# A first weight load issued third on GpSimd's queue, and the head's steps in a new order

## The chip, the cores and the metric

The program runs on one core of one Trainium2 chip. The metric is device time in microseconds (us) of one execution, smaller is better. Besides the plain times there is one execution taken by the hardware profiler; times inside it are counted from the start of its span.

## The reference, cut to what matters

There are two stages. The first is a sparse causal attention over 4 batches of 8 heads, 768 positions and 64 dimensions a head. Keys are taken in 24 chunks of 32. Each query gets an upper bound for each chunk from the chunk's smallest and largest key, keeps the 6 chunks with the highest bound, and attends to those alone:

```python
ub = np.sum(np.maximum(q[:, :, :, None, :] * k_min[:, :, None, :, :], q[:, :, :, None, :] * k_max[:, :, None, :, :]), axis=-1)
ub = np.where(causal, ub, -1000000000.0)
top_chunks = np.argsort(ub, axis=-1)[..., -top_k:]
mask = sel & (pos[:, None] >= pos[None, :])
scores = np.where(mask, scores, -1000000000.0)
attn = np.exp(scores - max);  attn = attn / sum;  out = attn @ v
```

The second stage is a soft mixture of experts over the 3072 x 512 result `x`: `logits = x @ phi` (32 slots); a softmax over all rows gives each slot its input, eight experts of two layers (`w1` 512 x 1024, relu, `w2` 1024 x 512) turn four slots each, and a softmax over the slots mixes the slot outputs back to the rows:

```python
d = softmax(logits, axis=0);  slot_input = d.T @ x
slot_out[e] = np.maximum(slot_input[e] @ w1[e], 0.0) @ w2[e]
return (softmax(logits, axis=1) @ slot_out).astype(np.float32)
```

## The kernel before, in words

Heads are worked on in 16 pairs, four to a batch. For a pair, q and k are transposed on TensorE (`transposes`, line 225), copied out of PSUM (`evac_T`, line 235), the chunk minima and maxima are reduced on VectorE (`kmin`, `kmax`, lines 244 and 250), spread over the two heads (`heads`, line 256; on VectorE as step `bd`, on GpSimd as step `bdp`), and multiplied with the negative and positive part of q (`qneg` line 264, `qpos` lines 272 and 274) to the upper bound (`ubound`, lines 284 and 294). `select` (lines 305 to 308) finds the sixth highest of each query with VectorE, with a small copy on GpSimd; the not-selected marks are transposed (`ns_transposes` line 316, `evac_ns` line 324) and added as a large negative number to the scores by matmuls (`scores`, lines 334 and 344). ScalarE takes the exponential (`expo`, line 358), in six groups `ex:0` to `ex:5`; groups 0, 1 and 4 have 1024 columns, the others 768. GpSimd zeroes what lies above the diagonal (`mask`, line 368). The product with v, the normalisation and the experts' stages come behind.

The program's order is written by hand. Pair 0, and the first steps of pairs 1 and 2, are the string `HEAD` (line 638), which is read word by word by `head` (line 640): each word issues its instructions, and each engine works its own instructions off in the order in which the words stand. The words: `w:n` issues n matmuls of 512 columns on a constant (`warm`, line 215) whose result nobody reads; `kd`, `ka`, `qd`, `qa` cast the two heads of pair 0's k and q on VectorE or ScalarE; `trk:i`, `trq:i` transpose, `evk:i`, `evq:i` copy out; `caus`, `qgrp`, `squad`, `identf`, `once` make constants on GpSimd, `schunk` on VectorE; `spreada` and `spreadp` fill the mask table on ScalarE and on GpSimd; `lk:i`, `lq:i` load k or q of the pairs i and i+1, `lv:i` loads v of pair i, `lw` the next of the expert weights, `phi` the slot matrix; `sc:g`, `ex:g`, `mk:g` are the score groups of pair 0. After `HEAD` a loop over pairs 1 to 15 reads a like string for each pair.

All loads but two are issued by GpSimd's queue, convert f32 to bf16 on their way, and land in the order in which they were issued; the two of pair 0 come from SyncE's queue (line 184) and don't convert. Loads of pair 1 and the constant `ident` stand ahead of `HEAD` (lines 185 to 190), as do the loads of pairs 2 and 3 (`load(2, ...)`, lines 202 and 203). Fourteen weight matrices of 1024 KB (`load_w`, line 150) are spread over the head and the loop; the last two matrices come as eight half pieces of 256 KB (`load_w_half`, line 160), the last four of them issued when the attention is done (line 859). The results leave by SyncE's queue: half of the columns (`out_half(m, 1, ...)`, line 1054) once the experts' first half is ready, the other half and the rest (line 1062 on) after the last weight pieces have been used (`last_expert_out`, line 1006).

Of the kernel before, what the change touches and what calls it, by code (L numbers as in the profile page):

```python
# [59 lines left out]
def kernel(  # L60
# [50 lines left out]
    identf = static.tile([P, P], F32, name="identf")  # L111
    ones_sq = static.tile([P, P], BF16, name="ones_sq")
    NJ = NQT // 2
    caus = static.tile([P, 1, 8], BF16, name="caus")
    qgrp = static.tile([P, 4, CH], BF16, name="qgrp")
    smask = static.tile([P, 2, NQT, 4, CH], BF16, name="smask")
    squad = static.tile([P, 2, 2, NCHUNK], BF16, name="squad")
    schunk = static.tile([P, 2, NCHUNK, 1], BF16, name="schunk")
# [23 lines left out]
    def load_w(i):  # L142

        if i < E:
            src = moe_w1[i].rearrange("(a p x) f -> p a (x f)", p=P, x=2)
            dst = w_sb[i].rearrange("p (a f) -> p a f", a=NDG // 2)
        else:
            src = moe_w2[LATE[i - E]].rearrange("(a p x) d -> p a (x d)", p=P, x=4)
            dst = w_sb[i].rearrange("p (a f) -> p a f", a=NFG // 4)
        nc.gpsimd.dma_start(out=dst, in_=src)  # L150
# [12 lines left out]
    def load(i, nm, n=1):  # L163

        b, j = divmod(i, NPB)
        t = ring[nm][i // 2 % 3][:, 2 * (i % 2):2 * (i % 2 + n)]
        src = {"k": k, "q": q}[nm][b, 2 * j:2 * (j + n)]
        nc.gpsimd.dma_start(out=t, in_=src.rearrange("h (p g) d -> p h (g d)", p=P))
        for x in range(n):
            st[nm, i + x] = t[:, 2 * x:2 * x + 2]  # L170
# [12 lines left out]
    for t, src in zip(stage, (k, q)):  # L183
        nc.sync.dma_start(out=t, in_=src[0, :2].rearrange("h (p g) d -> p h (g d)", p=P))
    load(1, "k")
    load(1, "q")
    nc.gpsimd.affine_select(
        out=ident, in_=ident, compare_op=ALU.not_equal, fill=1.0, base=0,
        pattern=[[-1, P]], channel_multiplier=1,
# [387 lines left out]
    once = static.tile([P, 8], BF16, name="once")  # L577
# [5 lines left out]
    def setup(name):  # L583
# [39 lines left out]
        elif name == "lw":  # L623
            load_w(LW.pop(0))
        else:
            return False
        return True

    LW = [0, 1]
    EVAC = {"evk": "k", "evq": "q"}  # L630
    CASTS = {"kd": (0, "k", 0, nc.vector.tensor_copy), "ka": (0, "k", 1, nc.scalar.copy),
             "qp": (1, "q", 0, nc.gpsimd.tensor_copy), "qd": (1, "q", 0, nc.vector.tensor_copy),
# [2 lines left out]
          "bdp": lambda i: heads(i, nc.gpsimd),  # L635
          "sel": select, "ns": ns_transposes, "evns": evac_ns, "lv": load_v}

    HEAD = """w:6 w:1 ka kd lv:0 caus qd qgrp trk:0 w:1 evk:0 qa trq:0 kmin:0 w:4 kmax:0 w:1 evq:0 lk:4 qsn:0 bd:0 squad schunk w:1 trk:1:s qsp:0 ub:0 w:1 spreada w:2 spreadp lw evk:1 w:1 sel:0 w:1 trq:1:s evq:1 ns:0 evns:0 sc:0 kmin:1 lv:1 kmax:1 lq:4 sc:1 lk:6 w:2 w:1 qsp:1 qsn:1 ex:0 sc:2 mk:0 w:1 ex:1 sc:3 ex:2 mk:2 bd:1 trk:2 ub:1 ex:3 mk:1 sel:1 sc:4 sc:5 evk:2 lq:6 kmin:2 mk:3 ex:4 trq:2 w:1 mk:4 once lv:2 ns:1 w:1 evns:1 w:1 evq:2 lw w:1 kmax:2 phi identf bd:2 qsn:2 ex:5 qsp:2"""

    def head(what):  # L640
        name, *arg = what.split(":")
        if setup(name):
            return
        if name in CASTS:
            cast(*CASTS[name])
            return
        i = int(arg[0])
        if name == "w":
            warm(i)
        elif name in ("trk", "trq"):  # L650
            runs = ((0, 3), (3, NQT)) if what == "trk:0" else ((0, NQT),)
            transposes(i, name[2], runs, (p_sc, "sc") if what == "trk:0" or arg[1:] else (p_tp, "tp"))
        elif name in EVAC:
            evac_T(i, EVAC[name], *((nc.scalar.copy, nc.vector.tensor_copy) if what == "evk:0" else ()))
        elif name in DO:
            DO[name](i)
        elif name in ("lk", "lq"):
            load(i, name[1], 2)
        elif name == "sc":
            scores(0, i)  # L660
        elif name == "ex":
            expo(0, i, False)
        elif name == "mk":
            mask(0, i)

    for what in HEAD.split():
        head(what)
# [442 lines left out]
```

## Time and profile before

| | us |
|---|---|
| median of 3 runs (lowest, highest) | 156.52 (156.43, 158.02) |
| the profiled execution's own time | 156.65 |
| its span | 154.9 |
| TensorE busy | 137.1 (89%) |
| ScalarE busy | 121.4 (78%) |
| VectorE busy | 120.3 (78%) |
| GpSimd busy | 97.3 (63%) |
| loads and stores, sum | 33.31 MB at a mean of 215 GB/s |

The profiled execution's time is 1.75 us longer than its span; the span is what the views divide up. A row of the timeline has start, duration, engine, line, operation, output<-inputs, shapes and count; in square brackets stands the idle time before it and what ended it. A row of DMA issues ends with the time from issue to landing. A row of the table of stretches has the stretch, its length, then the busy time of PE, PEld, DVE, ACT and POOL with their numbers of instructions, the granted clock of TensorE, the DMA engines' busy share (above 1 where transfers of one engine overlap) and GB/s moved.

### The profile page before, as it was taken

Reading aid. Unit: us, or ns where it says so; the run is one execution under the profiler, and the core shown is the slowest. Engines: PE = TensorE matmul, PEld = TensorE weight load, DVE = VectorE, ACT = ScalarE, POOL = GpSimd, SP = SyncE. Lnnn points to the kernel's source line nnn. Section 1 sums busy time; section 2 is a strip of 40 time slices with the busy share of each in tenths; the row PEclk is TensorE's granted clock in tenths of the full one; section 3 lists DMA queues with packets and bytes.
Section 4 is the critical chain, followed back from the end, with each engine's and each line's share of the span. In section 5 each row is a group of like instructions: output and inputs, shape, how many; then the busy total and the mean of one; then the engine's idle time right before and its main releaser. Section 6 shows DMA issues by size and latency. Waiting matters only on the chain.

```text
span 154.9 us, 6107 instructions
## 1 busy us (share of the span) xinstructions
PE 137.1 (89%) x2512; PEld 91.4 (59%) x2513; DVE 120.3 (78%) x445; ACT 121.4 (78%) x167; POOL 97.3 (63%) x200
## 2 busy tenths in 40 slices
PE   7999999999999999999999899999989899576700
PEld 2544566766767685766768566668768557353200
DVE  5866988989899998999999999999567532449800
ACT  3578999999999999999999989999977231527700
POOL 6976698965975898896649848793785950000000
PEclk9999999999999999999999999999999999999995
DMA  5999999999999999999999999999999999998995
GB/s 175 178 187 212 199 193 193 218 176 196 211 215 191 198 209 186 198 207 214 199 194 200 203 209 196 205 184 218 209 200 214 210 200 193 163 328 305 378 406 230
DMA packets 46171, 33.31 MB, mean 215 GB/s; under 512 B 26304, under 2 KB 41664, under 8 KB 46144
## 3 DMA queue, kind: packets, MB, share of 16 engines
q0 software_dynamic: 41328, 25.86, 115.2%
q1 hardware_dynamic: 4816, 7.08, 12.5%
q8 instruction: 19, 0.31, 0.7%
q14 instruction: 8, 0.07, 0.1%
HBM read 52.49 MB, written 6.29 MB: 379 GB/s over the span
## 4 chain that ended last, share of the span: by engine, by line
PE 65%; POOL 8%; DMA 7%; DVE 6%; ACT 5%; issue 4%; DVEq 0%; POOLq 0%; ACTq 0%
PE sc_ps L334 14%; PE at_ps L382 13%; PE sc_ps L344 10%; PE tr_ps L225 8%; DMA w_half<-in_moe_w_dram 7%; PE xT_ps L404 4%; PE warm_ps L215 3%; PE ub_ps L284 3%; ACT e_sb L358 3%; PE ns_ps L316 3%; DVE o_sb L1030 2%; POOL w_half L160 1%; POOL e_sb L368 1%; POOL v_t L174 1%; ACT o_sb L1027 1%
## 5 line engine op out<-in xcount | busy, mean ns | idle before, releaser
L358 ACT ACTIVATE e_sb<-sc_ps 128x1024 bf16<-128x1024 f32 (+2 forms) x96 | 83.2, 932 | 4.5 <-PE sc_ps L344 4.3
L368 POOL TENSOR_SCALAR_AFFINE_SELECT e_sb<-e_sb 128x256 bf16<-128x256 bf16 x96 | 37.8, 414 | 15.3 <-ACT e_sb L358 15.1
L334 PE MATMUL sc_ps<-qT,kT 64*128 64x384 bf16 (+3 forms) x260 | 37.5, 306 | 0.7 <-ACT e_sb L358 0.6
L344 PE MATMUL sc_ps<-nsT,smask 64*128 64x384 bf16 (+2 forms) x296 | 37.6, 284 | 0.1
L382 PE MATMUL at_ps<-v_t,e_sb 128*128 128x65 bf16 x630 | 26.0, 194 | 0.9 <-DVE x_sb L395 0.8
L382 PEld LDWEIGHTS <-e_sb 128*128 128x128 bf16 x630 | 22.1, 97 | 5.1 <-issue 3.9
L305 DVE MAX8 mx<-ub_ps 128x8 f32<-128x8 f32 (+1 forms) x192 | 16.9, 165 | 5.9 <-PE ub_ps L294 5.9
L334 PEld LDWEIGHTS <-kT 64*128 64x128 bf16 x260 | 13.5, 93 | 8.4 <-issue 1.8
L174 POOL DMA_DIRECT2D v_t<-in_v_dram x16 | 17.1, 1066 | 1.5 <-PE sc_ps L344 1.3
L344 PEld LDWEIGHTS <-smask 64*128 64x128 bf16 x296 | 14.9, 95 | 3.1 <-issue 0.4
L395 DVE TENSOR_TENSOR x_sb<-at_ps,inv 128x768 bf16<-128x768 f32 (+3 forms) x18 | 15.6, 869 | 0.6
L244 DVE TENSOR_REDUCE mm<-kT 128x24 bf16<-128x768 bf16 x16 | 15.1, 944 | 0.1
L250 DVE TENSOR_REDUCE mm<-kT 128x24 bf16<-128x768 bf16 x16 | 15.1, 943 | 0.0
L235 ACT COPY qT<-tr_ps 128x768 bf16<-128x768 bf16 x16 | 13.0, 814 | 2.2 <-PE tr_ps L225 2.2
L235 ACT COPY kT<-tr_ps 128x768 bf16<-128x768 bf16 (+1 forms) x16 | 12.7, 794 | 0.6 <-PE tr_ps L225 0.6
L150 POOL DMA_DIRECT2D w_sb<-in_moe_w_dram x14 | 10.1, 721 | 0.1
L415 DVE COPY xT_sb<-xT_ps 128x768 bf16<-128x768 bf16 (+1 forms) x16 | 8.6, 535 | 1.9 <-PE xT_ps L404 1.9
L215 PE MATMUL warm_ps<-ones_sq 128*128 128x512 bf16 x27 | 9.0, 458 | 1.1 <-DVE ones_sq L180 1.1
L284 PEld LDWEIGHTS <-qpn 128*128 128x128 bf16 x192 | 6.0, 96 | 4.5 <-issue 3.3
L404 PE MATMUL xT_ps<-ident,x_sb 128*128 128x128 bf16 x96 | 8.4, 220 | 0.0
L284 PE MATMUL ub_ps<-bd,qpn 128*128 128x48 bf16 x192 | 7.9, 184 | 0.4 <-issue 0.3
L1027 ACT ACTIVATE o_sb<-oh_ps,inv_a 128x256 f32<-128x256 f32 x12 | 5.0, 470 | 3.5 <-PE oh_ps L1041 2.8
(171 smaller groups left out, 222.5 us busy)
## 6 DMA issues: line engine op xcount, KB each, us to landing
w_sb<-in_moe_w_dram POOLq DMA_DIRECT2D x14, 1024.0 KB, 18.4
out_dram<-o_sb SPq DMA_DIRECT2D x14, 256.0 KB, 3.8
v_t<-in_v_dram POOLq DMA_DIRECT2D x16, 192.0 KB, 15.3
out_dram<-o_sb SPq DMA_DIRECT2D x5, 512.0 KB, 4.4
w_half<-in_moe_w_dram POOLq DMA_DIRECT2D x8, 256.0 KB, 11.8
k_in<-in_k_dram POOLq DMA_DIRECT2D x5, 384.0 KB, 13.4
q_in<-in_q_dram POOLq DMA_DIRECT2D x5, 384.0 KB, 12.2
w_sb<-in_k_dram POOLq DMA_DIRECT2D x2, 384.0 KB, 11.4
```

Source lines behind the costliest of these rows:

```text
L174: nc.gpsimd.dma_start(out=v_t[i % NV][:, :, :, :D], in_=v[b, 2 * j:2 * j + 2].rearrange("h (g p) d -> p h g d", p=P),)
L235: copy(t.rearrange("d (p g) -> d p g", g=NQT)[:, :, g0:g1], ps.rearrange("d g p -> d p g"),)
L244: nc.vector.tensor_reduce(mm[:, 0, 0, :], kT, axis=AX.X, op=ALU.min)
L250: nc.vector.tensor_reduce(mm[:, 1, 0, :], kT, axis=AX.X, op=ALU.max)
L284: nc.tensor.matmul(o, lhsT=qpn[:, x, t * P:(t + 1) * P], rhs=bd[:, x], start=(t == 0 and x == 0), stop=False,)
L305: nc.vector.max(mx[:, a, :], ub[:, a, :max(8, 4 * t + 4)])
L334: nc.tensor.matmul(ps[:, h, c:c + w], lhsT=kT[r, kg * P:(kg + 1) * P], rhs=qT[r, qs], start=True, stop=False,)
L344: nc.tensor.matmul(ps[:, h, c + (f - t0) * P:c + (l - t0) * P], lhsT=smask[r, x, kg].rearrange("p a b -> p (a b)"), rhs=nsT[r, (f - x * NJ ...
L358: nc.scalar.activation(e[:, :, :w], st.pop(("scps", i, g))[:, :, :w], func=ACT.Exp, scale=scale)
L368: nc.gpsimd.affine_select(out=e[:, :, c:c + P], in_=e[:, :, c:c + P], compare_op=ALU.is_ge, fill=0.0, base=0, pattern=[[0, 2], [1, P]], ch ...
L382: nc.tensor.matmul(o, lhsT=st["e", i, g][:, h, c:c + P], rhs=v_t[i % NV][:, h, kg, :D + 1], start=(kg == 0), stop=(kg == t),)
L395: nc.vector.tensor_tensor(st["x", b][:, t0:t1, 2 * j:2 * j + 2, :].rearrange("p t h d -> p h t d"), at[:, :, :, :D], inv.broadcast_to([P, ...
```

## The change

One weight load is moved from the word `lw` in the middle of `HEAD` to the third place of GpSimd's queue, and the words of `HEAD` get a new order, which also has more `w:` words, `bdp:1` in the place of `bd:1`, and the word `lw` once instead of twice.

```diff
     load(1, "k")
     load(1, "q")
+    load_w(0)
     nc.gpsimd.affine_select(
         out=ident, in_=ident, compare_op=ALU.not_equal, fill=1.0, base=0,
...
-    LW = [0, 1]
+    LW = [1]
...
-    HEAD = """w:6 w:1 ka kd lv:0 caus qd qgrp trk:0 w:1 evk:0 qa trq:0 kmin:0 w:4 kmax:0 w:1 evq:0 lk:4 qsn:0 bd:0 squad schunk w:1 trk:1:s qsp:0 ub:0 w:1 spreada w:2 spreadp lw evk:1 w:1 sel:0 w:1 trq:1:s evq:1 ns:0 evns:0 sc:0 kmin:1 lv:1 kmax:1 lq:4 sc:1 lk:6 w:2 w:1 qsp:1 qsn:1 ex:0 sc:2 mk:0 w:1 ex:1 sc:3 ex:2 mk:2 bd:1 trk:2 ub:1 ex:3 mk:1 sel:1 sc:4 sc:5 evk:2 lq:6 kmin:2 mk:3 ex:4 trq:2 w:1 mk:4 once lv:2 ns:1 w:1 evns:1 w:1 evq:2 lw w:1 kmax:2 phi identf bd:2 qsn:2 ex:5 qsp:2"""
+    HEAD = """w:1 kd w:3 ka w:7 trk:0 qa caus qgrp qd lv:0 lk:4 trq:0 evk:0 w:2 w:2 squad evq:0 w:2 qsp:0 w:1 kmin:0 kmax:0 bd:0 lv:1 w:1 qsn:0 w:1 trk:1:s trq:1 ub:0 w:1 schunk evq:1 spreada spreadp w:1 w:2 lq:4 evk:1 sel:0 w:3 ns:0 evns:0 qsn:1 sc:0 w:1 sc:1 ex:0 kmin:1 w:1 w:1 ex:1 w:1 qsp:1 kmax:1 w:3 bdp:1 trk:2 lk:6 evk:2 ub:1 sc:2 ex:2 sc:3 sel:1 identf mk:0 w:1 ex:3 once kmin:2 w:1 sc:4 kmax:2 trq:2 mk:2 lq:6 mk:1 ex:4 lv:2 evq:2 sc:5 mk:4 w:1 mk:3 ns:1 evns:1 bd:2 w:1 qsn:2 lw phi ex:5 qsp:2"""
```

## The prediction

> **What bounds the kernel now.** I read the page first, then the table of stretches, then the waits at the end. From the page, DMA busy share in 40 slices and GB/s:
>
> ```profile
> DMA  5999999999999999999999999999999999998995
> GB/s 175 178 187 212 199 193 193 218 176 196 211 215 191 198 209 186 198 207 214 199 194 200 203 209 196 205 184 218 209 200 214 210 200 193 163 328 305 378 406 230
> ```
>
> The stretches (last columns: granted clock, DMA share, GB/s):
>
> ```profile
> 2.00:137.90 135.90, 130.27 (x2472) 88.20 (x2471) 111.35 (x422) 114.08 (x155) 96.42 (x196) 1.00 1.35 203
> 140.00:141.00 1.00, 0.79 (x7) 0.40 (x5) 0.93 (x4) 0.93 (x3) 0.00 (x0) 1.00 0.50 177
> 141.00:153.00 12.00, 3.98 (x26) 1.64 (x24) 5.61 (x10) 4.41 (x8) 0.00 (x0) 0.89 1.02 383
> ```
>
> The reader is to see two bounds side by side. The DMA engines have work from 2.0 us to the last weight piece at 137.9, and then write results; TensorE is busy for 130.27 of those 135.90 us. Where they meet is seen in the chain in order of time and in TensorE's timeline:
>
> ```profile
> 127.27 10.62 DMA w_half<-in_moe_w_dram
> 132.54 0.29 PE L1006 MATMUL so_ps<-w_half,hT_pad 128*32 128x256 bf16 x4 [0.76 <-DMA w_half<-in_moe_w_dram]
> 137.94 0.29 PE L1006 MATMUL so_last<-w_half,hT_pad 128*32 128x256 bf16 x4 [0.32 <-DMA w_half<-in_moe_w_dram]
> ```
>
> TensorE waits for weight pieces twice, 0.76 and then 0.32 us. So the arithmetic may come 0.76 + 0.32 = 1.08 us later before the end moves, and coming earlier gains nothing while the loads last until 137.9. Behind that there is no slack: between 140 and 141 the DMA share is 0.50, the results' stream itself waits there for the arithmetic.
>
> **The change: the load stream.** A load lands in the order of issue, and the queue is already full when the moved load was issued. GpSimd's timeline and, below it, time from issue to landing of the loads of pairs 2 and 3 (k, then q), of v of pair 0 and of w:
>
> ```profile
> 3.21 0.79 POOL L168 DMA_DIRECT2D k_in<-in_k_dram  x1
> 3.97 0.77 POOL L168 DMA_DIRECT2D q_in<-in_q_dram  x1
> 4.70 1.19 POOL L174 DMA_DIRECT2D v_t<-in_v_dram  x1
> 9.10 0.74 POOL L150 DMA_DIRECT2D w_sb<-in_moe_w_dram  x1
> ```
> ```profile
> k_in<-in_k_dram POOLq DMA_DIRECT2D x1, 384.0 KB, 6.4
> q_in<-in_q_dram POOLq DMA_DIRECT2D x1, 384.0 KB, 7.5
> v_t<-in_v_dram POOLq DMA_DIRECT2D x1, 192.0 KB, 8.1
> w_sb<-in_moe_w_dram POOLq DMA_DIRECT2D x1, 1024.0 KB, 11.4
> ```
>
> The bytes are the same and the engines have had no hole for the earlier weight to fill, so the stream should end at 137.9 as before: 0 us, which holds as long as loads go on being issued ten us ahead (11.4 here, 10.62 for the last). What moves is who lands when. 1.05 MB at 203 GB/s put 5.2 us ahead of k, q and v: k of pairs 2 and 3 lands at 9.6 + 5.2 = 14.8, q at 16.7, v at 18.0. With 175 GB/s (first slice) or 218 (the fastest load slice) it is 6.0 or 4.8, k at 15.6 or 14.4; I take 5.2. GpSimd issues the weight in 0.74 us, so `ident` and all its later issues slip by that; their landings don't, with a backlog of 6.4 us, and `ident` is still ready before the first transpose.
>
> **The change: the order of the head.** TensorE, before:
>
> ```profile
> L215 PE MATMUL warm_ps<-ones_sq x7: 607/634/634, 1.1 to 3.7; 128*128 128x512 bf16 x7
> 4.24 0.95 PE L225 MATMUL tr_ps<-ident,k_in 128*64 128x128 bf16 x12
> 5.12 0.61 PE L215 MATMUL warm_ps<-ones_sq 128*128 128x512 bf16 x1
> 6.69 1.59 PE L215 MATMUL warm_ps<-ones_sq 128*128 128x512 bf16 x6
> 8.21 0.53 PE L225 MATMUL tr_ps<-ident,k_in 128*64 128x128 bf16 x12
> 8.67 0.47 PE L284 MATMUL ub_ps<-bd,qpn 128*128 128x48 bf16 x12
> L215 PE MATMUL warm_ps<-ones_sq x5: 376/377/379, 9.0 to 9.9; 128*128 128x512 bf16 x5
> 11.69 0.40 PE L344 MATMUL sc_ps<-nsT,smask 64*128 64x128 bf16 x4
> 15.00 0.47 PE L284 MATMUL ub_ps<-bd,qpn 128*128 128x48 bf16 x12
> 18.39 0.38 PE L344 MATMUL sc_ps<-nsT,smask 64*128 64x128 bf16 x4
> ```
>
> The warm matmuls start 0.43 us apart at first (2.6 / 6) and 0.22 later (0.9 / 4); twelve transposes take 0.88 (4.24 to 5.12), later 0.46 (8.21 to 8.67). The rate turns within the six that begin at 6.69. The granted clock reads 1.00 in all of this, so that column doesn't show it.
>
> Before, 7 warm matmuls stand ahead of `trk:0`, now 11: it starts at 1.1 + 11 x 0.43 = 5.85 in place of 4.24. `trk:0` (0.88) ends at 6.73, `trq:0`, across the turn, about 0.55 later, 7.3. Nine warm matmuls follow (6 before), 9 x 0.22 = 2.0, then `trk:1` and, newly ahead of `ub:0`, `trq:1`, 2 x 0.46: `ub:0` starts at 10.2, 1.5 later than at 8.67. VectorE, ScalarE and the small GpSimd step:
>
> ```profile
> 5.22 0.59 DVE L235 COPY kT<-tr_ps 128x384 bf16<-128x384 bf16 x1
> 5.93 0.95 DVE L244 TENSOR_REDUCE mm<-kT 128x24 bf16<-128x768 bf16 x1
> 7.92 0.25 DVE L256 TENSOR_TENSOR bd<-mm,headsel 128x96 bf16<-128x96 bf16 x1
> 11.28 0.36 DVE L324 COPY nsT<-ns_ps 128x384 bf16<-128x384 bf16 x1 [0.51 <-PE ns_ps L316]
> 14.02 0.24 DVE L256 TENSOR_TENSOR bd<-mm,headsel 128x96 bf16<-128x96 bf16 x1
> 16.65 0.46 DVE L308 TENSOR_TENSOR ns_t<-ub_ps,mx 128x288 bf16<-128x288 f32 x1
> L256 POOL TENSOR_TENSOR bd<-mm,headsel x6: 340/345/387, 58.6 to 98.5; 128x96 bf16<-128x96 bf16 x6
> 12.12 3.35 ACT L358 ACTIVATE e_sb<-sc_ps 128x1024 bf16<-128x1024 f32 x4 [0.56 <-PE sc_ps L344]
> 15.36 0.80 ACT L235 COPY kT<-tr_ps 128x768 bf16<-128x768 bf16 x1
> 17.70 0.83 ACT L358 ACTIVATE e_sb<-sc_ps 128x768 bf16<-128x768 f32 x1
> 18.81 2.02 ACT L358 ACTIVATE e_sb<-sc_ps 128x1024 bf16<-128x1024 f32 x2 [0.28 <-PE sc_ps L344]
> ```
>
> VectorE would be ready for `ub:0` earlier: its copy 0.98 after `trk:0` starts, `kmin` 0.71 on, and the four steps to `bd`'s end 2.24: 9.8. TensorE's words decide.
>
> From `ub:0` on the old distances hold: `evns:0` 2.6 later, 12.8; first exponential 3.45 later, 13.65 (12.12 before). In both orders five VectorE steps then stand ahead of pair 1's `bd`, 14.02 - 11.28 = 2.74, so 15.55; `bdp` on GpSimd 0.35 and two hand-overs, 16.0. Its queue is free then: `lq:4` is issued before, `lk:6` behind it. Beside this, TensorE has two score groups (from 13.2, 0.8 us) and six warm matmuls (1.3), so `trk:2` at 15.3 to 15.8, and k has landed (14.8): no wait, 0.3 us if it lands at 15.6. `ub:1` starts at 16.0, before 15.00.
>
> Now `sc:2` stands behind `ub:1` and so behind `bdp`; ScalarE, done with two exponentials at 15.5 and with `evk:2` at 16.6, idles until about 17.0. Before it ran eight pieces without a hole from 12.12 to 18.53, 6.4 us; less two exponentials (1.9) and `evk:2` (0.75), 3.8 us are left: pair 1's first exponential at 20.8. On VectorE's side, ns_t comes 1.65 after `ub:1`, 17.65, then `kmin:2`, `kmax:2` (0.9 each), now both ahead of `evns:1` at 19.8, score and exponential 0.9 later: 20.7. Before: 18.81. **The loop starts 1.9 us late.** pv's v (18.0) is there in time. GpSimd's queue doesn't add to it; its rows at the head's end, the mask's row from the costliest groups of the page:
>
> ```profile
> 17.17 0.77 POOL L168 DMA_DIRECT2D q_in<-in_q_dram  x1 [0.26 <-PE tr_ps L225]
> 23.51 0.27 POOL L307 CAST ns_t<-mx 128x12 bf16<-128x12 f32 x1
> L368 POOL TENSOR_SCALAR_AFFINE_SELECT e_sb<-e_sb 128x256 bf16<-128x256 bf16 x96 | 37.8, 414 | 15.3 <-ACT e_sb L358 15.1
> ```
>
> Before, it works from 17.17 (`lq:6`) to the next pair's small copy at 23.51 almost without a hole, 6.3 us, through two loads of v, one of w (the second, which stays there), phi's, three masks and constants. The new order has the same list and two masks more, 0.8, behind pair 1's copy at 17.8: 24.9, 1.4 late and so less than the 1.9.
>
> In the loop TensorE hardly idles, so it stays 1.9 late; what hides of it is 1.08. Sum: 0 (stream) + 1.9 - 1.08 = +0.8, and 156.65 + 0.8 = 157.4 us. The median shown, 156.52, is 0.13 lower than that execution.
>
> Bounds of the clock's turn, which no row shows for this order: had it been fast from the start, `ub:0` would come at about 8.1 and `ub:1` would wait for k (14.8 + 0.5 = 15.3): 1.2 late, +0.1 us. Slow through all 20 matmuls and four transposes, `ub:0` at 1.1 + 8.6 + 3.5 = 13.2: 4.9 late, +3.8 us. I take the turn where the rows have it, near 7.
>
> The Trainium skill, "TensorE: Matmul & The Clock Gate", Part 1 (the HAM clock gate), says that the clock rises after a busy window of about 3.4 us which runs freely, so not after a number of matmuls; as an estimate by that page the turn lies between 4.5 and 7.9 here, its middle makes `ub:0` 9.9 and the sum +0.5. The two rates above agree. Its Part 4 says that transposes don't count as busy in the same way; no row can show that, but it would make the unbroken run of eleven turn the clock earlier.
>
> **The rivals.** *The clock turns early.* The new run of matmuls is unbroken from 1.1 on, the old one is broken by transposes at 4.24. Turning at 5 or earlier gives +0.1 to +0.4: 156.8. Against it: before, 5.5 us of work were needed.
>
> *The clock turns late* (slower than before by over 1%). It costs 0.21 for each warm matmul that still runs slow. It decides from 158.1 on, that is when the loop is 2.5 late, three slow ones of the nine or a turn after about 8.3; with six of nine it is 157.4 + 1.3 = 158.7. For it: the earliest words hang on a rate seen in one execution only; against it: by 6.7 the old order had turned it.
>
> *The stream ends earlier.* If the head's loads packed better, the end could follow by what the results' stream idles, 0.5 us, and the arithmetic would have to be early too, which the head's sum denies. Faster by over 1% would need 1.6 us: 154.9.
>
> **Chances.** Forecast 0.50, early clock 0.24, late clock 0.22, earlier stream 0.04. One per cent is about what a measurement of this kernel can tell from no change (158.1 and 155.0); so faster 0.04, same 0.74, slower 0.22. The range, 156.4 to 158.9, holds the early clock less a little and most of the late one.
>
> **What would show it.** After: last weight piece still near 137.9; first k transpose near 5.9, `ub:0` near 10.2, pair 1's first exponential near 20.7; the 0.76 wait of so_ps gone, and a longer hole in the results' stream near 141. It is wrong if the stream's end moves, if TensorE stalls on k_in, or if the loop catches up.

## The result, and the profile after

The changed kernel takes 158.14 us (median of 20 runs, 156.99 to 159.9) against 156.93 for the kernel before on the same chip (20 runs, 156.16 to 158.25): a ratio of 1.0072, interval 1.0048 to 1.0096, so 1.1 us slower (the two medians are 1.2 apart). The profiled execution was the fastest of its 20 (156.99 us, span 155.3), only 0.34 above the profiled one of before. The pair of profiles thus shows a third of the loss; a second profile, further down, shows a larger one. A small part lies outside the span: the time less the span is 1.66 to 2.04 us in the 76 executions of the kernel before whose span is on record, and 1.69 to 2.95 (median 1.95) in the 20 of the changed kernel. No view divides that part up.

The page after, with its DMA rows in 40 slices, and the answers of the table of stretches (the columns are those of the stretches shown before):

```profile
DMA  4999999999999999999999999999999999989995
GB/s 151 208 211 200 181 194 193 216 178 195 215 213 190 198 209 187 198 209 214 197 193 203 198 214 194 205 187 215 209 203 213 211 194 198 153 281 345 376 404 230
```
```profile
2.00:137.36 135.36, 130.09 (x2451) 87.59 (x2453) 112.29 (x421) 114.38 (x155) 96.86 (x197) 1.00 1.35 202
136.00:138.00 2.00, 1.95 (x56) 1.66 (x59) 1.14 (x3) 1.21 (x4) 0.00 (x0) 1.00 0.88 269
138.00:139.00 1.00, 0.55 (x22) 0.27 (x12) 0.40 (x1) 0.00 (x0) 0.00 (x0) 1.00 0.82 281
140.00:141.00 1.00, 0.79 (x5) 0.44 (x5) 1.00 (x3) 0.99 (x4) 0.00 (x0) 1.00 0.99 347
```

The load stream has the same 1.35 share and 202 GB/s and ends at 137.36, 0.5 earlier, which buys nothing: the two waits for weight pieces are gone, and TensorE's late work ends the kernel. The hole in the results' stream, 0.50 at 140 before, now lies earlier (0.88 from 136 to 138, where it was 1.06 before, and 0.82 after that). TensorE's timeline, the head and then the last pieces:

```profile
5.33 0.53 PE L226 MATMUL tr_ps<-ident,k_in 128*64 128x128 bf16 x12
...
6.16 2.12 PE L216 MATMUL warm_ps<-ones_sq 128*128 128x512 bf16 x9
...
9.02 0.47 PE L285 MATMUL ub_ps<-bd,qpn 128*128 128x48 bf16 x12
...
15.25 0.47 PE L285 MATMUL ub_ps<-bd,qpn 128*128 128x48 bf16 x12
...
21.50 0.45 PE L285 MATMUL ub_ps<-bd,qpn 128*128 128x48 bf16 x11 [0.28 <-DVE qpn L275]
...
45.31 0.39 PE L335 MATMUL sc_ps<-qT,kT 64*128 64x512 bf16 x2 [0.27 <-ACT e_sb L359]
...
130.91 0.61 PE L971 MATMUL so_ps<-w_sb,hT_pad 128*32 128x256 bf16 x16
...
133.26 0.39 PE L1007 MATMUL so_ps<-w_half,hT_pad 128*32 128x256 bf16 x8
...
138.16 0.39 PE L1007 MATMUL so_last<-w_half,hT_pad 128*32 128x256 bf16 x8
...
139.14 0.61 PE L1042 MATMUL oh_ps<-so_all,cT_all 128*128 128x256 bf16 x4 [0.59 <-DVE so_all L1062]
```

The rows that answer to the last four in the kernel before:

```profile
129.15 0.61 PE L970 MATMUL so_ps<-w_sb,hT_pad 128*32 128x256 bf16 x16
...
131.50 0.28 PE L1006 MATMUL so_ps<-w_half,hT_pad 128*32 128x256 bf16 x4
...
137.33 0.28 PE L1006 MATMUL so_last<-w_half,hT_pad 128*32 128x256 bf16 x4
...
138.82 0.61 PE L1041 MATMUL oh_ps<-so_all,cT_all 128*128 128x256 bf16 x4 [0.59 <-DVE so_all L1061]
```

From the start of so_ps to the `oh_ps` of the second half it is 139.14 - 130.91 = 8.23 us after and 138.82 - 129.15 = 9.67 before. In ten of the 14 profiles this stretch is 8.23 or 8.24; the other four wait for a weight piece in it, one of them at half the clock as well. So the kernel before held **1.44 us of waiting** here, not the 1.08 printed in the two brackets. The difference is in how a wait is printed: four matmuls take 0.28 and eight take 0.39, so the second four would have started 0.11 after the first four, at 131.61 and 137.44. They started at 132.54 and 137.94: 0.93 and 0.50 late. The brackets count only from the modelled end of the matmuls in flight. So a delay of 1.76 at so_ps becomes 0.32 at `oh_ps`, and 0.34 in the time.

Time from issue to landing of the loads in question after (the weight, then k and q of pairs 2 and 3):

```profile
w_sb<-in_moe_w_dram POOLq DMA_DIRECT2D x1, 1024.0 KB, 9.6
k_in<-in_k_dram POOLq DMA_DIRECT2D x1, 384.0 KB, 10.5
q_in<-in_q_dram POOLq DMA_DIRECT2D x1, 384.0 KB, 12.6
```

Issued at about 3.9 and 4.7, k and q land at 14.4 and 17.2. ScalarE's timeline after; the row contains pair 1's first exponential, which begins at 20.05 (18.81 before):

```profile
19.35 2.66 ACT L359 ACTIVATE e_sb<-sc_ps 128x768 bf16<-128x768 f32 x3
```

The loop begins 1.24 us late and is 1.77 late at the last pair.

### The profile page after: what moved, and what is told of

The parts are those of the page before. It is cut to its first block, busy times and chain, and to the rows that moved or that the text cites. A ratio compares the mean times of both kernels' runs of the same rounds, so it can differ in the third digit from the quotient of the medians.

```text
span 155.3 us, 6133 instructions
## 1 busy us (share of the span) xinstructions
PE 137.9 (89%) x2523; PEld 91.5 (59%) x2524; DVE 121.2 (78%) x444; ACT 121.7 (78%) x167; POOL 97.7 (63%) x201
## 4 chain that ended last, share of the span: by engine, by line
PE 54%; POOL 12%; ACT 9%; DVE 7%; issue 6%; DMA 6%; DVEq 0%; POOLq 0%; ACTq 0%
PE sc_ps L335 12%; PE at_ps L383 11%; PE sc_ps L345 8%; ACT e_sb L359 6%; PE tr_ps L226 6%; DMA w_half<-in_moe_w_dram 6%; PE xT_ps L405 3%; POOL v_t L174 3%; PE ub_ps L285 3%; POOL e_sb L369 2%; ACT o_sb L1028 2%; PE ns_ps L317 2%; DVE o_sb L1031 2%; PE warm_ps L216 2%; POOL w_sb L168 2%
## 5 line engine op out<-in xcount | busy, mean ns | idle before, releaser
L174 POOL DMA_DIRECT2D v_t<-in_v_dram x16 | 17.2, 1073 | 0.2 <-issue 0.2
L216 PE MATMUL warm_ps<-ones_sq 128*128 128x512 bf16 x38 | 11.3, 435 | 1.1 <-DVE ones_sq L180 1.1
L309 DVE TENSOR_TENSOR ns_t<-ub_ps,mx 128x288 bf16<-128x288 f32 x16 | 7.3, 457 | 0.5
```

The source lines that it names most:

```text
L174: nc.gpsimd.dma_start(out=v_t[i % NV][:, :, :, :D], in_=v[b, 2 * j:2 * j + 2].rearrange("h (g p) d -> p h g d", p=P),)
```

## The experiments

In the text below, "late" is the first exponential of a pair against the same one in the profile of before. A new order's words are given only where they differ.

**The two parts alone.** First the weight issued third, with the old order of words:

```diff
+    load_w(0)
...
-    LW = [0, 1]
+    LW = [1]
...
-w:2 spreadp lw evk:1
+w:2 spreadp evk:1
```

> The kernel before with one part of the change alone: the first weight is issued third, the words of the head keep their old order (the first lw is gone). Theory A (the order of the words delays the arithmetic, the load stream ends when it did): k of pairs 2 and 3 lands near 14.4 and q near 17.2 as in the changed kernel, so TensorE waits up to 1 us at trq:2 (16.3 before), the loop starts 0.5 to 1 us late, and that hides in the waits at the end: ratio to before 1.000 to 1.002, last weight piece within 0.6 us of 137.9. Rival B (the weight's place costs the time): at least the 1.0072 of the whole change, 1.006 to 1.010. Rival C (the early weight shortens the load stream and the order spoils it): below 0.998.

Measured 156.63 us, ratio 0.9986 (0.9958 to 1.0014): no cost. TensorE's timeline of this kernel:

```profile
17.33 0.53 PE L226 MATMUL tr_ps<-ident,q_in 128*64 128x128 bf16 x12 [0.90 <-DMA q_in<-in_q_dram]
...
130.12 0.61 PE L971 MATMUL so_ps<-w_sb,hT_pad 128*32 128x256 bf16 x16
```

The late q does stall TensorE, by 0.90 us, and the loop stays 0.8 to 1.0 late to its end (so_ps 0.97). All of that hides. Then the new order alone, with the weight in its old place:

```diff
-    load_w(0)
...
-    LW = [1]
+    LW = [0, 1]
...
-spreada spreadp w:1
+spreada spreadp lw w:1
```

> The changed kernel with its new order of words, but the first weight issued in the middle of the head again, behind spreadp, as before. Theory A: ratio to before 1.005 to 1.009, nearly that of the whole change; the loop starts 1.0 to 1.3 us late. k of pairs 2 and 3 lands near 9.6 again, and TensorE's k transposes of pair 2 stay where six warm matmuls put them, near 14.8. Rival B (the weight's place): 0.999 to 1.003.

Measured 158.38, ratio 1.0070 (1.0038 to 1.0103). The order of words by itself carries the whole loss.

```profile
9.96 0.47 PE L284 MATMUL ub_ps<-bd,qpn 128*128 128x48 bf16 x12
...
132.18 0.61 PE L970 MATMUL so_ps<-w_sb,hT_pad 128*32 128x256 bf16 x16
...
140.41 0.61 PE L1041 MATMUL oh_ps<-so_all,cT_all 128*128 128x256 bf16 x4 [0.59 <-DVE so_all L1061]
```

TensorE's timeline here has a delay of 3.03 at so_ps, of which 1.44 hides: `oh_ps` is 1.59 late. The loop starts 2.44 late, more than the 1.0 to 1.3 expected; the rate turned at 6.76 here, and at 4.65 in the first profile of the changed kernel, whose loop starts 1.24 late.

**The changed kernel once more,** unedited, with a profile of its own.

> The changed kernel once more, beside the others on the same chip. The ratio 1.0072 should come back within 0.003. Its profile is a second draw of when TensorE's matmuls turn fast (4.8 us in the first profile, 6.9 in that of before): by theory D (the moment of the turn makes the changed kernel's runs differ and is the reason why its profiled run was only 0.34 us above that of before while the medians differ by 1.2) a profile with a turn at 6 or later has ub:0 at 9.8 or later in place of 9.0, and a span longer by the same amount less what hides at the end; by its rival (the spread comes from elsewhere) the span does not follow the turn.

Measured 158.61 (6 runs), ratio 1.0117 (1.0078 to 1.0156): further from 1.0072 than the 0.003 expected, though the two intervals overlap. TensorE's timeline and one stretch of its profile:

```profile
5.93 0.85 PE L226 MATMUL tr_ps<-ident,k_in 128*64 128x128 bf16 x12
...
7.14 2.12 PE L216 MATMUL warm_ps<-ones_sq 128*128 128x512 bf16 x9
...
9.98 0.47 PE L285 MATMUL ub_ps<-bd,qpn 128*128 128x48 bf16 x12
...
16.06 0.47 PE L285 MATMUL ub_ps<-bd,qpn 128*128 128x48 bf16 x12
...
133.02 0.61 PE L971 MATMUL so_ps<-w_sb,hT_pad 128*32 128x256 bf16 x16
```
```profile
126.00:130.00 4.00, 4.00 (x53) 1.98 (x56) 1.81 (x9) 1.19 (x3) 3.21 (x6) 0.57 1.41 190
```

Here the transposes are slow at 5.93 (0.85 for twelve) and the nine matmuls fast at 7.14: the rate turned near 7, where the working had put it, while in the first profile it was fast by 5.33 (0.53). The trace's record of the granted clock begins at that moment: at 6.84 here, at 4.65 in the first profile and at 6.97 in that of before. Pair 1 starts 2.04 late (20.85), and the last pair is 2.86 late. The 1.0 more at so_ps came from a granted clock of 0.57 from 126 to 130, in the experts' stage. Such a dip is not what the change costs: four of the 14 profiles have one ahead of the last results, one of them with the old order (four matmuls more, below), and a granted clock under 0.97 on average over the execution stands in 26 of 76 executions of the kernel before and in 4 of 20 of the changed one.

**How much hides at the end.** Extra matmuls that nobody reads, put in the stage ahead of so_ps of the kernel before; here nine, the others differ by the number.

```diff
-    keep(1)
+    keep(10)
```

> The kernel before with four more matmuls of 480 columns that nobody reads, ahead of the experts' first matmuls, about 0.8 us of TensorE. It measures what hides at the end. Theory: the two waits for weight pieces (0.76 and 0.32 us) take it: ratio to before 0.999 to 1.002. Rival (the results' stream has no slack and every delay counts): 1.004 to 1.006.

> As before with nine such matmuls, about 1.8 us, as much as the changed kernel's arithmetic is late at that place. Theory: 1.08 to 1.44 us of it hide, +0.4 to +0.8 us: ratio 1.002 to 1.005. Rival (no slack): 1.010 to 1.013.

> As before with eighteen such matmuls, about 3.7 us. Theory: all but 1.1 to 1.4 us counts, +2.3 to +2.7 us: ratio 1.014 to 1.018. Rival (the loads hide more than that, the end is set by the stream alone): below 1.008.

Measured 1.0026 (0.9997 to 1.0054), 1.0045 (1.0013 to 1.0077) and 1.0245 (1.0205 to 1.0284). With nine:

```profile
131.02 0.61 PE L970 MATMUL so_ps<-w_sb,hT_pad 128*32 128x256 bf16 x16
...
138.71 0.29 PE L1006 MATMUL so_last<-w_half,hT_pad 128*32 128x256 bf16 x4 [0.16 <-DMA w_half<-in_moe_w_dram]
```

TensorE's timeline shows so_ps 1.87 late; the last weight piece landed 0.8 later than before and still holds TensorE for 0.16, so that `oh_ps` is 0.77 late, and the time rises by 0.7 us. With four, the profile has a clock dip as well: so_ps is 1.97 late and `oh_ps` 0.53, so 1.44 hides again. The ratio with four lies between the two expectations and decides nothing; that with nine excludes the rival without slack, that with eighteen the rival in which the loads hide more. So a delay counts from a threshold on, as two bounds give it.

The eighteen cost 3.8 us, above both expectations, where 18 x 0.21 - 1.44 = 2.3 was due. Its profile has two further delays. The first is pair 0's q, which landed at 6.87 (4.78 before); VectorE cast it late and TensorE waited, so the loop is 1.48 late throughout:

```profile
7.31 0.67 PE L225 MATMUL tr_ps<-ident,q_in 128*64 128x128 bf16 x12 [1.56 <-DVE q_in L581]
```

The second is behind `oh_ps`: the last results landed 15.25 us after the second half's first result was issued, in place of 14.1. That stands in three other profiles too: the order alone, and two further down (the third score group first, pair 2's v late). These four, and none of the ten others, have one load of the program's own instructions more within the span. From the pages of eighteen and of before:

```profile
q8 instruction: 20, 0.33, 0.7%
```
```profile
q8 instruction: 19, 0.31, 0.7%
```

The traces put the start of this load of 16 KB at 146.4 to 147.5 us, while results are written, and at that place two results land 1.9 us apart (elsewhere at most 1.4). That it holds them up is likely but was not tested, and what sets it off is open.

**The two halves of the new order.** The first: the new words up to `ub:0`, then the old ones, weight in its old place.

```diff
-w:6 w:1 ka kd lv:0 caus qd qgrp trk:0
...
+w:1 kd w:3 ka w:7 trk:0 qa caus qgrp qd lv:0 lk:4 trq:0 evk:0 w:2 w:2 squad evq:0 w:2 qsp:0 w:1
+kmin:0 kmax:0 bd:0 lv:1 w:1 qsn:0 w:1 trk:1:s trq:1 ub:0
```

> The kernel before, weight in its old place, with the new order up to and including ub:0 (eleven warm matmuls first, nine between, trq:1 ahead of ub:0) and the old order behind it. Theory E (the loss is a sum of two halves, each of which alone would mostly hide in the waits at the end): ub:0 at 9.0 if TensorE turns fast by 5 us, near 10.0 if it turns near 7; all that follows is late by the same 0.4 to 1.3 us and no more; about 1 to 1.4 us hide: ratio to before 1.000 to 1.003. Rival F (the eleven and nine warm matmuls are the whole loss): 1.006 to 1.010. Rival G (only the words behind ub:0 cost): 0.998 to 1.000.

Measured 157.21, ratio 1.0000 (0.9967 to 1.0033). The second: the old words up to `ub:0`, then the new ones.

```diff
-ub:0 w:1 spreada w:2 spreadp lw evk:1
...
+ub:0 w:1 trq:1:s evq:1 spreada spreadp lw w:1 w:2 lq:4 evk:1 sel:0 w:3 ns:0 evns:0 lv:1 qsn:1 sc:0 w:1
+sc:1 ex:0 kmin:1 w:1 w:1 ex:1 w:1 qsp:1 kmax:1 w:3 bdp:1 trk:2 lk:6 evk:2 ub:1 sc:2 ex:2 sc:3
...
```

> The other half: the old order up to ub:0, behind it the new one (third score group and its exponential behind pair 1's bound, kmin:2 and kmax:2 ahead of evns:1, bd of pair 1 on GpSimd, six warm matmuls ahead of trk:2), weight in its old place. Theory E: ub:0 at 8.7 with a turn near 7, ub:1 near 15.0 to 15.2, pair 1's first exponential 0.9 to 1.2 us later than before, and it stays so; ratio to before 1.000 to 1.003. Rival G (this half is the whole loss): 1.006 to 1.010. Rival F: 0.998 to 1.000.

Measured 157.65, ratio 1.0009 (0.9977 to 1.0041). By these ratios neither half costs anything that can be measured, and both together cost 0.7%. By the plain medians the halves are 0.2 and 0.7 us above the kernel before (156.99), and the order as a whole, run on another chip, 1.6 (156.79 there). The so_ps rows of the first half, with a stretch behind it, and of the second:

```profile
130.03 0.61 PE L970 MATMUL so_ps<-w_sb,hT_pad 128*32 128x256 bf16 x16
```
```profile
136.00:138.00 2.00, 2.00 (x35) 1.24 (x36) 0.86 (x2) 0.87 (x2) 0.00 (x0) 0.50 0.89 253
```
```profile
130.67 0.61 PE L970 MATMUL so_ps<-w_sb,hT_pad 128*32 128x256 bf16 x16
...
138.91 0.61 PE L1041 MATMUL oh_ps<-so_all,cT_all 128*128 128x256 bf16 x4 [0.59 <-DVE so_all L1061]
```

They are 0.88 and 1.52 late in TensorE's timelines, each near or under 1.44; the second's `oh_ps` is 0.09 late. The first's profile can't show what hides, for the granted clock fell to 0.50 behind so_ps and `oh_ps` came 1.53 late; that execution took 158.27, above the half's median. Together the two delays exceed 1.44: 0.88 + 1.52 - 1.44 = 1.0, near the 1.1 of the whole change. This is the plainest test of the mechanism: the same delays are nearly free one by one and not in sum.

**What sets the head's delay.** Four fewer warm matmuls ahead of the first transpose:

```diff
-ka w:7 trk:0
+ka w:3 trk:0
```

> The changed kernel with 7 instead of 11 warm matmuls ahead of the first transposes, as many as before. Theory A with the clock's turn: k transposes of pair 0 start at 4.3 to 4.5 instead of 5.3 to 5.9, ub:0 at 8.2 to 9.0, and the loop starts up to 0.5 us earlier than in the changed kernel, not more, since then k of pairs 2 and 3 (14.4) holds TensorE: ratio to before 1.002 to 1.005. Rival (the warm matmuls ahead of the first transposes don't matter, the delay comes from the words behind ub:0): 1.006 to 1.009, as the whole change.

Measured 158.91, ratio 1.0111 (1.0069 to 1.0153): nothing gained, and more than either expectation. In its profile the first transpose started earlier, at 4.95 behind a wait of 0.65 for VectorE's cast of k, but the rate turned later; TensorE's timeline:

```profile
6.51 3.63 PE L216 MATMUL warm_ps<-ones_sq 128*128 128x512 bf16 x9
```

These nine take 2.12 in both profiles of the changed kernel. Here the rate turned only at 9.62, near their end, and `ub:0` came at 10.87. Then the nine taken out:

```diff
-evk:0 w:2 w:2 squad evq:0 w:2 qsp:0 w:1 kmin:0 kmax:0 bd:0 lv:1 w:1 qsn:0 w:1 trk:1:s
+evk:0 squad evq:0 qsp:0 kmin:0 kmax:0 bd:0 lv:1 qsn:0 trk:1:s
```

> The changed kernel without the nine warm matmuls between trq:0 and trk:1. Theory (they hold ub:0 when TensorE turns fast late): VectorE's chain sets ub:0, at 8.5 to 9.3 us, and the loop starts 0.3 to 1 us earlier than in a changed kernel with the same turn; ratio to before 1.003 to 1.007, below the 1.0117 that the changed kernel had on one chip and near the 1.0072 of the other. Rival (TensorE needs that work to turn fast; without it the turn comes at 9 us or later, as with four warm matmuls less, where it came near 9.6): slow transposes and bounds for longer, ratio 1.009 or more.

Measured 158.83, ratio 1.0093 (1.0057 to 1.0129): a miss, no gain either. The ratio is the rival's, but not for the rival's reason: the rate turned at 6.06. TensorE's timeline tells why:

```profile
7.59 0.53 PE L226 MATMUL tr_ps<-ident,k_in 128*64 128x128 bf16 x12 [0.76 <-DMA k_in<-in_k_dram]
8.63 0.53 PE L226 MATMUL tr_ps<-ident,q_in 128*64 128x128 bf16 x12 [0.51 <-DMA q_in<-in_q_dram]
9.78 0.47 PE L285 MATMUL ub_ps<-bd,qpn 128*128 128x48 bf16 x12 [0.63 <-DVE qpn L265]
```

With TensorE free, the loads of pair 1 and then VectorE's chain hold `ub:0` at 9.78, which is the 9.8 of the working. The nine covered waits of the same length. Then pair 0's third score group ahead of pair 1's steps:

```diff
-kmax:1 w:3 bdp:1 trk:2 lk:6 evk:2 ub:1 sc:2 ex:2 sc:3
+kmax:1 sc:2 ex:2 bdp:1 trk:2 lk:6 evk:2 ub:1 sc:3
```

> The changed kernel with the third score group and its exponential (sc:2 ex:2) put ahead of pair 2's k transposes and pair 1's bound instead of behind them, and the three warm matmuls there left out. Theory A (ScalarE's idle 0.8 us in front of evk:2, and a third exponential that stands behind bdp, are a part of the loop's late start): ScalarE's hole at 14.6 to 15.4 closes, the loop starts 0.5 to 0.9 us late instead of 1.24, ratio to before 1.001 to 1.004. Rival (VectorE's chain to evns:1 sets the start of the loop, ScalarE's hole is covered): the loop's start stays within 0.2 us of the changed kernel's, ratio 1.006 to 1.009.

Measured 158.26, ratio 1.0093 (1.0056 to 1.0130): no gain, and it doesn't test the idea well, for k of pairs 2 and 3 landed at 15.55 in its profile and held the next transpose:

```profile
15.60 0.53 PE L226 MATMUL tr_ps<-ident,k_in 128*64 128x128 bf16 x12 [0.90 <-DMA k_in<-in_k_dram]
```

**Why the delay grows in the loop.** In every profile with the order's second half, but for the one below that moves a load, lateness rises by 0.2 or more at pair 2, and in all of them by 0.3 at pair 5. With the weight alone it rises by 0.19 at pair 2. VectorE beside GpSimd in the profile of after:

```profile
19.40 0.62 DVE L257 TENSOR_TENSOR bd<-mm,headsel 128x96 bf16<-128x96 bf16 x1
19.95 1.02 DVE L265 TENSOR_SCALAR qpn<-qT 128x768 bf16<-128x768 bf16 x1
```
```profile
19.39 0.42 POOL L369 TENSOR_SCALAR_AFFINE_SELECT e_sb<-e_sb 128x256 bf16<-128x256 bf16 x1
19.74 1.04 POOL L174 DMA_DIRECT2D v_t<-in_v_dram  x1
20.80 1.26 POOL L369 TENSOR_SCALAR_AFFINE_SELECT e_sb<-e_sb 128x256 bf16<-128x256 bf16 x3
```

The two VectorE steps, 0.25 and 0.35 at their shortest, take 0.62 and 1.02. Beside the first GpSimd works on a mask to 19.81, beside the second it issues a load of v to 20.78. TensorE then waits 0.28 for the VectorE step behind them (at 21.50 above). So that issue was moved to the end of the head:

```diff
-ex:4 lv:2 evq:2
+ex:4 evq:2
...
-ex:5 qsp:2
+ex:5 qsp:2 lv:2
```

> The changed kernel with the load of pair 2's v issued at the end of the head instead of beside pair 2's qsn and qsp on VectorE. In the changed kernel qsn:2 took 1.02 us instead of 0.35 and bd:2 0.62 instead of 0.26, while GpSimd issued that load and masked. Theory (GpSimd's issuing of a load holds up VectorE's copies of that kind): qsn:2 is back at 0.35 to 0.55 and TensorE's wait of 0.28 us for it ahead of pair 2's bound is gone; the loop's late start changes by at most 0.3 us, ratio 1.005 to 1.012. Rival (the stretch has another cause): qsn:2 stays near 1.0.

```profile
20.34 0.25 DVE L257 TENSOR_TENSOR bd<-mm,headsel 128x96 bf16<-128x96 bf16 x1
20.50 0.57 DVE L265 TENSOR_SCALAR qpn<-qT 128x768 bf16<-128x768 bf16 x1
```

VectorE's timeline has 0.57 in place of 1.02, a little above the range expected: a mask runs beside this step. The first growth is gone (2.17 late at pair 1, 2.09 at pair 2). The time doesn't show it: 159.82 in 4 runs, ratio 1.0139 (1.0075 to 1.0204), above the 1.012 expected, and with so few runs not told apart from the changed kernel. A fifth of a us is below what these runs tell, and this profile's clock dipped too. That the issue alone can hold VectorE, without a mask, stands in the kernel with the weight alone, whose TensorE waits 0.34 us for this step of VectorE, beside a load of v that GpSimd issues from 19.74 to 20.80:

```profile
20.08 0.87 DVE L275 TENSOR_SCALAR qpn<-qT 128x768 bf16<-128x768 bf16 x1
```

Not every issue does it: in the profile of after the same two kinds of step take 0.26 and 0.35 at 8.44 and 8.61, under the issue of another v. What makes the difference no run shows.

The second growth is TensorE's wait at 45.31 above, for an exponential that itself waited 0.31 us for a mask of GpSimd; ScalarE's timeline of after:

```profile
44.45 3.35 ACT L359 ACTIVATE e_sb<-sc_ps 128x768 bf16<-128x768 f32 x4 [0.31 <-POOL e_sb L369]
```

The same wait stands with the second half alone and not with the first half or the weight alone. Why that mask is late for it was not tried.

## Why the prediction was right, step by step

**What held.** The sign of the result held, and the time came 0.7 above the forecast, inside the range. The load stream: predicted to end unchanged, it ended between 137.2 and 138.7 in all profiles, and the weight's move alone costs nothing. The head: in the profile where the rate turned near 7, `ub:0` started at 9.98 (10.2 predicted), `ub:1` at 16.06 (16.0) and pair 1's first exponential at 20.85 (20.7 to 20.8). VectorE's alternative for `ub:0`, 9.8, was measured as 9.78. The 0.76 wait is gone. The result is then the delay less what hides.

**What was mis-sized.** Three terms. First, what hides is 1.44, not 1.08: the printed idle time understates it, as shown above. Second, the step "in the loop TensorE hardly idles, so it stays 1.9 late" failed: lateness grew by 0.5 to 0.8, a fifth of a us of it through VectorE beside a mask and the issue of v, the rest at pair 5 and later. The working had looked at when GpSimd's queue comes free (24.9; 25.32 in the second profile), and put at nothing what its masks and loads do to VectorE meanwhile. Third, q landed at 17.2 and 17.9 in the two profiles, not 16.7; k (14.4 and 15.0) had the bounds given. The first two pull opposite ways: 2.86 - 1.44 = 1.4 in the second profile without its clock dip, 0.8 predicted, 1.1 measured. With the measured terms the forecast's own case would have been 156.65 + 1.4 = 158.1, the median. That 157.4 fell only 0.7 short is in part luck: the two errors offset each other to some extent, and clock dips and late results, about 1 us each in single executions, were in no term. The hole in the results' stream was expected near 141 and lay from 136 to 139, because the first half's results are late as well.

**The rivals.** The earlier stream didn't come. Of the clock's turn, both early and usual cases occurred with the same kernel: near 4.7 in the first profile, which gave 156.99 (156.8 was its price), and near 7 in the second. So these two are not alternatives but draws, and they are likely a part of why the changed kernel's runs spread from 156.99 to 159.9; only two of these runs have a profile. The late turn appeared once, near 9.6, with four warm matmuls fewer. The working's price of 0.43 for each warm matmul ahead of `trk:0` is no rule for edits: it held as a distance between two rows, but fewer of them didn't make `ub:0` earlier.

The Trainium skill, "TensorE: Matmul & The Clock Gate", Part 1, counts the warm-up in time and not in matmuls. The runs agree: by the traces' clock records the turn lay between 4.4 and 7.1 in the seven profiles with eleven unbroken matmuls, and between 4.4 and 7.0 in six of the seven profiles with seven; once it was 9.6. Two turns, 4.39 and 4.44, lie a little ahead of the 4.5 to 7.9 that was estimated by that page. The one with 9.6 lies far behind it; no run shows why.

What stays open: why the mask at pair 5 is late, what brings the additional load of instructions beside which the last results of four profiles landed over a microsecond later, and what the time outside the span is. No version tried beats the kernel before; the weight alone equals it in time.

## What to carry to other kernels

Where two streams meet at the end, a delay in one costs only what exceeds its wait at the meeting point, so parts that are free one by one can cost in sum: test them both alone and together. Read that slack as a distance between starts, with and without the wait, because the idle time printed beside a pipelined matmul is too short (1.08 for 1.44 here). And compare a profiled execution with the median before reading a pair of profiles: here it was the fastest of 20.

## What the runs showed of the hardware

The granted clock reads 1.00 while the first matmuls run 0.43 us apart; the trace has no record of it before the turn, so the slow start is to be read from the spacing. It does show drops: 0.57 from 126 to 130 in the changed kernel's second profile (0.50 for 3.4 us in the trace), which cost about 1 us. The same stage in the first profile of the same kernel ran at 1.00.

A VectorE step took 1.02 for 0.35 us while GpSimd issued a load (0.57 with the issue moved away), and another 0.62 for 0.25 while GpSimd worked on a mask for most of it. The Trainium skill, "SBUF — State Buffer", section "SBUF: two separate sides", says that VectorE and GpSimd share a pair of ports that one instruction holds to its end, and warns that VectorE then delays GpSimd's loads. The mask's row agrees with the first; the load's rows show the opposite direction of the second, VectorE delayed by the issue of a load (1.02, and 0.87 with the weight alone), and two steps that were not (0.26 and 0.35).

In four profiles of 14 the last results landed 15.25 to 15.45 us after the first of their half was issued, in place of 14.1 to 14.6, and just these four have a 16 KB load of instructions between 146.4 and 148.4 us. Whether it is the cause was not tried.
